# A first sequence in blocks of 112 consecutive tokens: convolution by tap matrices and a router in the same layout

## Chip, cores, metric

One core of one Trainium2 chip. The metric is the device time of one execution in microseconds (us). Chips differ: the first comparison ran on a chip where the kernel before takes 1368 us; of the three chips of the experiments, chip 11 takes the same 1368, chips 2 and 10 take 1382 to 1383. Each experiment is therefore held against runs of the kernel before on its own chip.

## The reference, cut

```python
# 8 sequences of 3584 tokens, 192 channels; depthwise causal convolution,
# 7 taps, one set of taps per head of 24 channels
w = exp(w - max(w)); w = w / (sum(w) + 1e-9)
y[b, s, h] = sum_k w[h, k] * x_pad[b, s + k, h]
# mixture of 8 experts; a token takes over the expert of the token before it
logits = y @ w_gate
local  = sigmoid(y @ w_local)
e = argmax(logits[s]) if s == 0 or local[s] < 0.5 else e_of_token(s - 1)
out[s] = softmax(logits[s])[e] * (relu(y[s] @ w1[e]) @ w2[e])
```

## The kernel before: the parts concerned

The 28,672 tokens are cut into 16 groups of 1792; two groups are one sequence. A group is convolved and routed, its rows are scattered to slots sorted by expert, and a loop over blocks of slots reads them back, multiplies and scatters the results. Before the loop come groups 0 and 1. There a partition holds 14 tokens in a row; four of eight heads are convolved by TensorE with diagonal matrices, one matmul per tap, the rest by VectorE.

```python
for i, h in enumerate(ON_PE):                     # 4 heads x 7 taps
    for k in range(KC):
        ...                                       # cut: i == 0, the same on VectorE
        nc.scalar.activation(dg_of(i, k), ident, Act.Copy, scale=c[:, h, k:k + 1])
...
for k in range(KC):                               # 28 matmuls of 336 columns
    nc.tensor.matmul(acc, lhsT=dg_of(i, k), rhs=chans(h, k),
                     start=(k == 0), stop=(k == KC - 1))
...
for k in range(1, KC):                            # the other heads
    nc.vector.scalar_tensor_tensor(cols(h), chans(h, k), c[:, h, k:k + 1],
                                   cols(h), Alu.mult, Alu.add)
```

The loop; `step(t)` issues about `t` us of VectorE work for later groups (convolution, router):

```python
xT, _ = turn(blocks[0][1], xgs[0])                # transposes of slot rows
for i, (_, n, _, _) in enumerate(blocks):
    ensure(i)                                     # slot rows ahead
    weights(i + AHEAD)                            # expert weights ahead
    hT = hidden(n, wbs[i], xT)                    # H_i
    xT, copied = turn(blocks[i + 1][1], xgs[i + 1])
    ...                                           # cut: a scatter of a later group
    step(2.5 if n == 1 else 4.2)
    output(n, wbs.pop(i), xgs.pop(i), hT)         # O_i, then step(1.2), then o_sb
    step(1.3 if n == 1 else 3.0)
```

`output` takes two PSUM tiles (PSUM is the memory that matmuls write to); the next `output` can start only when VectorE's `o_sb` has read them, and VectorE works in program order.

Of the kernel before, what the change touches and what calls it, by code (L numbers as in the profile page):

```python
# [17 lines left out]
P = 128  # L18
# [6 lines left out]
NT = 14  # L25
# [3 lines left out]
NP = NT // 2  # L29
HALO = KC - 1  # L30
NX = NT + HALO
# [24 lines left out]
GQ = (NP + 3) // 4  # L56
# [17 lines left out]
def taps(nc, scr, w):  # L74

    wm = scr.tile([1, H], F32, name="wm")
    nc.vector.tensor_reduce(wm, w, axis=AX.X, op=Alu.max)
    nc.vector.tensor_tensor(w, w, bcast(wm, KC), op=Alu.subtract)
    nc.scalar.activation(w, w, Act.Exp)
    ws = scr.tile([1, H], F32, name="ws")  # L80
    nc.vector.tensor_reduce(ws, w, axis=AX.X, op=Alu.add)
    nc.vector.tensor_scalar(ws, ws, 1e-9, None, Alu.add)
    nc.vector.reciprocal(ws, ws)
    nc.vector.tensor_tensor(w, w, bcast(ws, KC), op=Alu.mult)


@with_exitstack
def kernel(
    ctx: ExitStack,
    tc: tile.TileContext,  # L90
    x: bass.AP,
    weight: bass.AP,
    wgl: bass.AP,
# [31 lines left out]

    ident = cst.tile([P, P], F32, name="ident")
    ones = cst.tile([P, P], F32, name="ones")
    c = cst.tile([P, H, KC], F32, name="c")
    with tc.tile_pool(name="scr", bufs=1) as scr:
        w = scr.tile([1, H, KC], F32, name="w")  # L130
        nc.scalar.dma_start(out=w, in_=weight.rearrange("(o h) k -> o h k", o=1))
        x_in = {0: load_x(0)}
        nc.gpsimd.memset(ones, 1.0)
        any_ = scr.tile([1, 1], F32, name="any_")
        nc.scalar.activation(any_, ones[:1, :1], Act.Exp)
        make_identity(nc, ident)
        taps(nc, scr, w)
        cps = hps_p.tile([P, GQ * P], F32, name="hps")
        nc.tensor.matmul(cps[:, :H * KC], lhsT=ones[:1, :], rhs=w.rearrange("o h k -> o (h k)"),
                         start=True, stop=True)  # L140
        nc.vector.tensor_copy(c.rearrange("p h k -> p (h k)"), cps[:, :H * KC])
    wg = cst.tile([P, 3 + DQ, Q], F32, name="wg")
    nc.sync.dma_start(out=wg.rearrange("p k e -> p (k e)"), in_=wgl)
    wgq = wg[:, 3:, :]
    x_in[1] = load_x(1)


    HEADS = [5, 6, 7, 0, 1, 2, 3, 4]
    ON_PE = HEADS[:4]
    got = {}  # L150


    diag = wp.tile([P, WA + WB], F32, name="wb")

    def dg_of(i, k):
        n = i * KC + k
        return diag[:, n * P:(n + 1) * P] if n < 24 else more[:, (n - 24) * P:(n - 23) * P]

    more = wp.tile([P, WA + WB], F32, name="wb")
    for i, h in enumerate(ON_PE):  # L160
        for k in range(KC):
            if i == 0:
                nc.vector.tensor_scalar(dg_of(i, k), ident, c[:, h, k:k + 1], None, Alu.mult)
            else:
                nc.scalar.activation(dg_of(i, k), ident, Act.Copy, scale=c[:, h, k:k + 1])

    def conv(g, x_sb, on_pe=(), alone=False):

        y_sb = ys.tile([P, NT, DG], F32, name="y_sb")
        got[g] = y_sb  # L170

        def cols(h):
            return y_sb[:, :, Y0 + h * GS:Y0 + (h + 1) * GS]

        def chans(h, k):
            return x_sb[:, k:k + NT, h * GS:(h + 1) * GS]

        def first(h):
            if alone:
                nc.vector.tensor_scalar(cols(h), chans(h, 0), c[:, h, 0:1], None, Alu.mult)  # L180
            else:
                nc.scalar.activation(cols(h), chans(h, 0), Act.Copy, scale=c[:, h, 0:1])  # L182

        def others():
            for i, h in enumerate(on_pe):
                cps = (yps_p.tile([P, 512], F32, name="yps") if g else
                       hps_p.tile([P, 512], F32, name="hps"))
                acc = cps[:, :NT * GS]
                for k in range(KC):
                    nc.tensor.matmul(acc, lhsT=dg_of(i, k), rhs=chans(h, k),  # L190
                                     start=(k == 0), stop=(k == KC - 1))
                    if k == KC - 1:
                        nc.scalar.copy(cols(h), acc.rearrange("p (t d) -> p t d", d=GS))
                    yield

        def mine():
            hs = [h for h in HEADS if h not in on_pe]
            if not alone:
                first(hs[0])
                yield 0  # L200
            for i, h in enumerate(hs):
                if alone:
                    first(h)
                elif i + 1 < len(hs):
                    first(hs[i + 1])
                for k in range(1, KC):
                    nc.vector.scalar_tensor_tensor(cols(h), chans(h, k), c[:, h, k:k + 1],  # L207
                                                   cols(h), Alu.mult, Alu.add)
                    yield 0.6

        return mine(), others()

    for gen in reversed(conv(0, x_in.pop(0), ON_PE, True)):
        for _ in gen:
            pass
# [23 lines left out]
    i_of = pf[:, 0:1]  # L239
    so_far = cst.tile([1, P + 1], F32, name="so_far")  # L240
    nc.gpsimd.memset(so_far, 0.0)
    lsb = cst.tile([P, GQ * P], F32, name="lsb")
# [6 lines left out]
    for zero in (lsb, rk, bk, mk, mc, tq):  # L249
        nc.gpsimd.memset(zero, 0.0)  # L250
# [32 lines left out]
    def wide_logits(g, y_sb):  # L283

        zy = yt.tile([P, NT * DR + 12 * 2 * P], F32, name="z")
        yr = zy[:, :NT * DR].rearrange("p (t d) -> p t d", d=DR)
        yT = zy[:, NT * DR:].rearrange("p (u j x) -> p u j x", u=3, j=4)

        copy = nc.scalar.copy if g else nc.gpsimd.tensor_copy
        copy(yr, y_sb[:, :, Y0 + P:Y0 + D])  # L290
        if not g:
            copy(y_sb[:, :, Y0 + D:], y_sb[:, :, Y0:Y0 + DR])



        for u in range(3):
            tps = [hps_p.tile([P, 4 * GQ, DR], F32, name="hps") for half in range(2)]
            for j in range(4):
                for q in range(GQ):
                    t = min(2 * (4 * q + j), NT - 2)  # L300
                    src = (yr[:, t:t + 2, :].rearrange("p t d -> p (t d)") if u == 2
                           else y_sb[:, t + u, Y0:Y0 + P])
                    for half in range(2):
                        turn_half(tps[half][:, GQ * j + q, :], src, half)
            for half in range(2):
                to = yT[:, u, :, :].rearrange("p j (q s) -> p (j q) s", q=GQ)
                leave = nc.vector.tensor_copy if g == 0 and half else nc.scalar.copy
                leave(to[:, :, half * DR:(half + 1) * DR], tps[half])
        lps = hps_p.tile([P, 2 * P], F32, name="hps")
        for u in range(3):  # L310
            for j in range(4):
                w = (2 if 4 + j < NP else 1) * P
                nc.tensor.matmul(lps[32 * j:32 * j + 32, :w], lhsT=wg[:, u, :],
                                 rhs=yT[:, u, j, :w], start=(u == 0), stop=(u == 2))
        m = 32 * (NP - 4)
        nc.scalar.copy(lsb[:m, :], lps[:m, :])
        nc.scalar.copy(lsb[m:, :P], lps[m:, :P])
        if g:
            copy(y_sb[:, :, Y0 + D:], y_sb[:, :, Y0:Y0 + DR])
        yield "hop"  # L320
        ltp = [hps_p.tile([P, GQ, 2, 32], F32, name="hps") for half in range(2)]
        for q in range(GQ):
            for half in range(2):
                turn_half(ltp[half][:, q, :, :].rearrange("p j e -> p (j e)"),
                          lsb[:, q * P:(q + 1) * P], half)
        lt = sm.tile([P, NT + 2, E + 1], F32, name="lt")
        yield "pe"
        for half in range(2):
            nc.vector.tensor_copy(
                lt.rearrange("p (q h j u) e -> p q h j (u e)", q=GQ, h=2, u=2)[:, :, half, :, :],  # L330
                ltp[half][:, :, :, :2 * (E + 1)])
        return lt

    def logits(g, y_sb):

        nc.gpsimd.tensor_copy(y_sb[:, :, Y0 + D:], y_sb[:, :, Y0:Y0 + DR])
        zy = yt.tile([P, NT * DR + 12 * 2 * P], F32, name="z")
        z = zy[:, :NT * D].rearrange("p (t d) -> p t d", d=D)
# [32 lines left out]

    def route(g, alone):
        y_sb = got.pop(g)
        lt = yield from (wide_logits if alone else logits)(g, y_sb)
        lg = lt[:, :NT, :E]
        mx = sm.tile([P, NT], F32, name="mx")
        nc.vector.tensor_reduce(mx, lg, axis=AX.X, op=Alu.max)
# [169 lines left out]
        if ONE[g] > (ONE[was] if g else 0):  # L547
            yield from table(0, g, 1, ONE[g])
# [415 lines left out]
```

## Time and profile before

| | kernel before |
|---|---|
| time, median of the first 3 runs | 1368.14 us |
| span of the profiled run | 1366.1 us |
| TensorE (PE) busy from 330 us on | 1029.4 of 1030 us |
| slot numbers of group 0 (T0) | 46.7 us |
| first hidden products H0 | 71.6 us |
| second output products O1, third hidden products H2 | 84.7, 87.4 us |

How to read it: from 330 us on PE has no gap, so a change of the part before the loop can move the end only by what it changes before 330 us. What is called "lead" below is the difference of two traces in the start of the same copy of a transposed block (there are 142 copies, one per block), each counted from its span's start. The trace lists each matmul here as two records, which the counts (x32) count.

The waits of PE between 75 and 130 us show what disturbs these first blocks (columns: engine, line, releaser, us in total, times, longest). Slot rows come late by 3.6 us, and nothing waits for VectorE's `o_sb`:

```profile
PE xps L279 <- DMA xg<-slots: 3.6, 2, 2.4
PE yps L760 <- issue: 1.7, 1, 1.7
```

### The profile page before, as it was taken

The page shows a single profiled execution, that of the slowest core. Times are in us where ns is not written, and L with a number is a line of the kernel's source. Part 1 is how long each engine was busy: PE and PEld are TensorE (multiplying, and loading weights), DVE is VectorE, ACT ScalarE, POOL GpSimd, SP SyncE. Part 2 cuts the span into 40 slices and gives each one's busy share as a digit, 9 for nine tenths or more (in the row PEclk, how much of TensorE's full clock was granted, in tenths as well). Part 3 has the DMA queues.
Part 4 walks back from the last instruction along what each step waited for, and adds up shares of the span by engine and source line. Part 5 has one row for each costly group of instructions (what it writes and reads, how often), then busy time and mean ns, then how long its engine had stood idle before and what let it go on. Part 6 is the DMA issues. An engine that isn't in the chain of part 4 may idle for free. (4 is left out here: it accounts for less than half of the span.)

```text
span 1366.1 us, 41871 instructions
## 1 busy us (share of the span) xinstructions
PE 1327.2 (97%) x17142; PEld 1252.3 (92%) x17142; DVE 795.1 (58%) x2459; ACT 512.1 (37%) x1146; POOL 481.2 (35%) x513
## 2 busy tenths in 40 slices
PE   6789999999999999999999999999999999999998
PEld 4488999999999999999999999999999999999997
DVE  6778999988878777878686868684500000000000
ACT  3243444434333333333343434333333333333333
POOL 1442444434343434344444344443343111112111
PEclk9989999999999999999999999999999999999999
DMA  4399999996675757676767676565566555556893
GB/s 181 102 375 374 374 390 373 359 353 251 235 273 206 267 208 265 213 264 219 264 228 265 223 266 220 208 211 208 212 221 224 202 196 181 181 178 235 318 325 131
DMA packets 65812, 340.75 MB, mean 249 GB/s; under 512 B 12369, under 2 KB 23240, under 8 KB 45395
## 3 DMA queue, kind: packets, MB, share of 16 engines
q1 hardware_dynamic: 43488, 285.35, 57.8%
q0 software_dynamic: 22128, 52.70, 10.2%
q8 instruction: 136, 2.23, 0.7%
q14 instruction: 58, 0.47, 0.1%
q10 hardware_dynamic: 2, 0.00, 0.0%
HBM read 285.20 MB, written 53.29 MB: 248 GB/s over the span
## 5 line engine op out<-in xcount | busy, mean ns | idle before, releaser
L760 PE MATMUL yps<-wb,hT 64*128 64x192 f32 x7328 | 636.9, 325 | 3.7 <-DVE o_sb L772 2.0
L744 PE MATMUL hps<-xT,wb 64*128 64x256 f32 (+1 forms) x6816 | 630.4, 337 | 0.8 <-ACT xT L730 0.6
L760 PEld LDWEIGHTS yps<-wb,hT 64*128 64x128 f32 x7328 | 599.7, 187 | 8.5 <-issue 4.5
L744 PEld LDWEIGHTS hps<-xT,wb 64*128 64x128 f32 x6816 | 567.1, 188 | 41.5 <-issue 1.1
L776 POOL DMA_INDIRECT out_dram<-o_sb,xg x229 | 231.5, 1011 | 664.3 <-DVE o_sb L772 591.6
L207 DVE SCALAR_TENSOR_TENSOR y_sb<-x_sb,c,y_sb 128x336 f32<-128x336 f32 x720 | 406.2, 573 | 28.5 <-ACT y_sb L182 9.3
L749 ACT ACTIVATE hT<-hps 128x512 f32<-128x512 f32 (+1 forms) x568 | 261.3, 512 | 361.2 <-PE hps L744 361.0
L772 DVE SCALAR_TENSOR_TENSOR o_sb<-yps,xg,o_sb 128x192 f32<-128x192 f32 x229 | 87.2, 412 | 488.6 <-ACT o_sb L768 488.6
L567 POOL DMA_INDIRECT slots<-y_sb,posi x224 | 222.7, 994 | 185.7 <-ACT hT L749 92.2
L768 ACT ACTIVATE o_sb<-yps,xg 128x192 f32<-128x192 f32 x229 | 87.0, 419 | 420.6 <-PE yps L760 417.0
L730 ACT COPY xT<-xps 128x768 f32<-128x768 f32 (+1 forms) x142 | 96.7, 681 | 11.6 <-PE xps L279 11.6
L279 PEld LDWEIGHTS xps<-ident,xg 64*128 64x128 f32 x1374 | 71.2, 140 | 13.8 <-issue 3.9
L279 PE MATMUL xps<-ident,xg 64*128 64x64 f32 x1374 | 72.5, 222 | 5.8 <-DMA xg<-slots 5.8
L182 ACT ACTIVATE y_sb<-x_sb,c 128x336 f32<-128x336 f32 x116 | 66.7, 586 | 0.0
L341 DVE STREAM_TRANSPOSE z<-y_sb 128x768 f32<-128x768 f32 (+1 forms) x56 | 45.5, 853 | 0.5
L367 DVE COPY lt<-lq 32x36 f32<-32x36 f32 x224 | 41.6, 186 | 3.5
L351 PE MATMUL hps<-z,wg 64*32 64x128 f32 x1344 | 26.7, 274 | 1.4 <-DVE z L341 1.3
L351 PEld LDWEIGHTS hps<-z,wg 64*32 64x32 f32 x1344 | 20.7, 105 | 5.0 <-DVE z L341 3.0
L190 PE MATMUL hps<-x_sb,wb 128*128 128x336 f32 x56 | 18.9, 506 | 4.0 <-DMA x_sb<-in_x_dram 4.0
L190 PEld LDWEIGHTS hps<-x_sb,wb 128*128 128x128 f32 x56 | 12.1, 218 | 10.5 <-issue 6.2
L190 PE MATMUL yps<-x_sb,wb 128*128 128x336 f32 x56 | 16.8, 451 | 0.0
L190 PEld LDWEIGHTS yps<-x_sb,wb 128*128 128x128 f32 x56 | 10.3, 190 | 4.5
(165 smaller groups left out, 336.0 us busy)
## 6 DMA issues: line engine op xcount, KB each, us to landing
wb<-in_w_dram SPq DMA_DIRECT2D x142, 1536.0 KB
x_sb<-in_x_dram SPq DMA_DIRECT2D x16, 1920.0 KB
xg<-slots SPq DMA_DIRECT2D x87, 258.0 KB
xg<-slots SPq DMA_DIRECT2D x55, 129.0 KB
out_dram<-o_sb,xg POOLq DMA_INDIRECT x229
slots<-y_sb,posi POOLq DMA_INDIRECT x224
wg<-in_wgl_dram SPq DMA_DIRECT2D x1, 144.0 KB
slots<-pad SPq DMA_DIRECT2D x1, 129.0 KB
```

The lines of the kernel that those rows point to most:

```text
L182: nc.scalar.activation(cols(h), chans(h, 0), Act.Copy, scale=c[:, h, 0:1])
L190: nc.tensor.matmul(acc, lhsT=dg_of(i, k), rhs=chans(h, k), start=(k == 0), stop=(k == KC - 1))
L207: nc.vector.scalar_tensor_tensor(cols(h), chans(h, k), c[:, h, k:k + 1], cols(h), Alu.mult, Alu.add)
L279: nc.tensor.transpose(to, src[rows], identity=ident[rows, rows])
L567: ins = nc.gpsimd.indirect_dma_start(out=slots[:, :], in_=rows, in_offset=None, out_offset=bass.IndirectOffsetOnAxis(ap=to, axis=0)).ins
L730: copied = nc.scalar.copy(to, at)
L744: nc.tensor.matmul(hps[half][:, j, w], lhsT=wb[rows, f0:f0 + P], rhs=xT[rows, d, w], start=(d == 0 and j == 0), stop=(d == KD - 1), skip_g ...
L749: relu = nc.scalar.activation(hT[:, m:m + 2, w], hps[half][:, :, w], Act.Relu)
L760: nc.tensor.matmul(yps[half][:, k * D:(k + 1) * D], lhsT=hT[rows, m, k * P:(k + 1) * P], rhs=wb[rows, WA + m * D:WA + (m + 1) * D], start= ...
L768: nc.scalar.activation(o_sb[:, k, :], y[k][0], Act.Copy, scale=xg[:, k, 0:1])
L772: nc.vector.scalar_tensor_tensor(o_sb[:, k, :], y[k][1], xg[:, k, 0:1], o_sb[:, k, :], Alu.mult, Alu.add)
L776: sent = nc.gpsimd.indirect_dma_start(out=out, in_=o_sb[:, k, :], in_offset=None, out_offset=bass.IndirectOffsetOnAxis(ap=xg.bitcast(I32)[ ...
```

## The change

Intent: both groups of the first sequence in blocks of 112 consecutive tokens, 16 blocks side by side, a block's tokens along the partitions. A convolution of one head is then one product with a 118x112 tap matrix in place of seven with diagonal matrices, and no head is left to VectorE; the router's scans run along rows. The tap matrices come from the host as unnormalized logarithms (-1e30 off the band) and are exponentiated on chip. Further, ahead of the loop, `step(15)` starts group 2's convolution on VectorE. Core of the diff:

```diff
+        nc.scalar.dma_start(out=hank, in_=wh)          # tap matrices, second queue
+        x_in = {0: load_b(0)}                          # x in blocks, two halves
...
+        for h in range(H):
+            nc.scalar.activation(hank[:, h, :], hank[:, h, :], Act.Exp, bias=nm[:, h:h + 1])
+        ... normalization: exp(w), sums, 1/sums on VectorE, then a matmul that spreads them
+        nc.tensor.matmul(cps[:, :H + H * KC], lhsT=ones[:1, :], rhs=ws, start=True, stop=True)
+        nc.vector.tensor_copy(rz, cps[:, :H])
...
-    for gen in reversed(conv(0, x_in.pop(0), ON_PE, True)):
+        for b0 in (0, NH):
+            for h in range(H):                         # 16 matmuls of 192 columns a group
+                nc.tensor.matmul(ps, lhsT=hank[:NI, h, :],
+                                 rhs=xv[:NI, b0:b0 + NH, h * GS:(h + 1) * GS],
+                                 start=True, stop=True)
...  (cut: logits with whole transposes, router along rows, 16 scatters a group in place of 14)
+    for _ in wide_route(1, yb, acc[1]):
+        step(1.2)
-    for _ in range(4):
+    for _ in range(6):
         put()
+    step(15)
     AHEAD = 3
```

## The prediction

> **What bounds the kernel now.** I read, in this order, the page's slices, the busy time by stretch, TensorE's waits by stretch, and the timeline of the first 130 us. The chain that ended last is of no use: it holds only the last output scatter (0.1%).
>
> The slices come first. TensorE (PE) is at 9 from the fourth slice on; only the first three (34 us each) have room. GpSimd and ScalarE are never near full; DMA is at 9 in slices 3 to 8.
> ```profile
> PE   6789999999999999999999999999999999999998
> DVE  6778999988878777878686868684500000000000
> PEclk9989999999999999999999999999999999999999
> DMA  4399999996675757676767676565566555556893
> ```
> Next the stretches (start:end, then busy us of PE, PE weight load, VectorE, ScalarE, GpSimd, then clock, DMA share, GB/s). After 330 us PE is busy 1029.4 of 1030 us, and its waits there list nothing: that stretch only shifts. Between 62 and 76 us PE is mostly idle or at half clock.
> ```profile
> 62.00:72.00 10.00, 2.76 (x15) 1.98 (x17) 8.34 (x43) 0.78 (x2) 4.18 (x5) 0.51 0.53 159
> 72.00:76.00 4.00, 4.00 (x40) 4.00 (x40) 1.02 (x8) 0.66 (x2) 3.00 (x4) 0.51 0.94 360
> 76.00:82.00 6.00, 6.00 (x98) 5.94 (x94) 2.55 (x5) 3.04 (x8) 2.52 (x3) 1.00 1.01 397
> 330.00:1360.00 1030.00, 1029.38 (x13003) 978.44 (x13000) 515.98 (x1617) 380.70 (x804) 350.41 (x352) 1.00 0.65 230
> ```
> So the end is set by when the expert loop starts and by PE's stalls early in it. The timeline (start, duration, engine, line) gives the chain to the loop: convolution from 8.67, logits from 28.19, slot numbers of group 0 (`posi`) at 46.56, fourteen scatters from 47.67 to 64.61, the read of the slots at 68.41, the first transposes at 70.48, the first hidden product at 71.64.
> ```profile
> 8.67 18.94 PE L190 MATMUL hps<-x_sb,wb 128*128 128x336 f32 x56 [3.98 <-DMA x_sb<-in_x_dram]
> 28.19 1.22 PE L279 MATMUL hps<-ident,y_sb 64*128 64x64 f32 x32 [0.57 <-issue]
> 46.56 0.17 DVE L539 CAST posi<-pos 128x14 int32<-128x14 f32 x1
> 47.67 1.27 POOL L567 DMA_INDIRECT slots<-y_sb,posi  x1 [18.58 <-issue]
> 64.61 0.96 POOL L567 DMA_INDIRECT slots<-y_sb,posi  x1 [0.30 <-issue]
> 68.41 1.19 SPq L697 DMA_DIRECT2D xg<-slots  x2
> 70.48 0.59 PE L279 MATMUL xps<-ident,xg 64*128 64x64 f32 x6 [2.27 <-DMA xg<-slots]
> 71.64 4.98 PE L744 MATMUL hps<-xT,wb 64*128 64x128 f32 x48 [0.57 <-ACT xT L730]
> 79.94 0.42 DVE L772 SCALAR_TENSOR_TENSOR o_sb<-yps,xg,o_sb 128x192 f32<-128x192 f32 x1 [1.19 <-ACT o_sb L768]
> 80.28 5.87 DVE L207 SCALAR_TENSOR_TENSOR y_sb<-x_sb,c,y_sb 128x336 f32<-128x336 f32 x10
> 84.51 0.40 PE L279 MATMUL xps<-ident,xg 64*128 64x64 f32 x6 [2.37 <-DMA xg<-slots]
> 84.72 2.85 PE L760 MATMUL yps<-wb,hT 64*128 64x192 f32 x32
> ```
> Call posi's end T0 (46.7 before) and the k-th block's hidden products Hk, its output products Ok. Undisturbed, a block takes 5.52 us (H8 to H9, 126.98 to 132.49). H0 to H7 (71.64 to 121.43) took 49.8 us instead of 7x5.52+1.9 (logits of group 2)=40.5: about 9 us of stalls and half clock.
>
> **What the Trainium skill says.** "TensorE: Matmul & The Clock Gate", Part 1: after an idle window of about 3.4 us PE falls to half clock and needs about as long a busy one to return. The trace agrees in part: H0 took 4.98 us at 0.51, H1 2.84 at full clock. But PE was at full clock at 8.67, after eight idle microseconds. Same page, Part 2, "Step-by-step": MATMULs stay in program order, only weight loads are pulled ahead; the trace shows it where O1 waits behind the transposes at 84.51. "ScalarE: Activation LUTs", "What ACT_TABLE_LOAD costs": an ACTIVATE with a pointer operand takes 280 ns + 0.833 ns per element and overlaps its neighbour by 93 ns; at 128 columns an estimated 294 ns, and the trace has 21 in 6.24 us (297 ns).
>
> **The change, part by part.** Groups 0 and 1 (one sequence, 3584 tokens) both get the new layout. In the main loop the instruction orders of both kernels hold the same products and logits; what changes is the prologue and where group 2's convolution lies.
>
> *Taps.* The tap matrices (459 KB, second queue) and half of x (786 KB) come together. Before, 1.92 MB of x landed at 8.5 us; by share of bytes I estimate 5.7 for the taps. Then, on one chain: 8 exponentials of 112 columns at 0.28 (2.25), the exponential of w (0.25), four small VectorE operations (0.9 as at 3.03 to 3.91 before), hops (0.2), a matmul (0.67). This matmul is ahead of the convolution in PE's order, so the convolution starts at 10.0, later than before (8.67), and its evacuation needs `rz` at 10.3.
>
> *Convolution of group 0.* 28 matmuls of 336 columns (0.555 each on PE, 18.9 us with VectorE's share beside) become 16 of 192: 0.555x192/336=0.32, say 0.33; 5.3 us. Evacuation by two engines, about 0.35 each, keeps pace. Done at 15.3 against 27.6.
>
> *Logits.* 24 whole transposes in lots of four (0.5 us a lot, estimated from 32 half ones in 1.22), evacuation 0.45 to 0.5 a lot, wide products 1.8 per half, then copies, four transposes, one copy: about 7.8 us; the 8.4 before (28.1 to 36.5) were similar. Logits at 23.1.
>
> *Router.* 33 VectorE operations; spaced as in the undisturbed chain of group 1 before (61.47 to 69.61), 9.3 us. Group 1's convolution lies between on PE; of the four PSUM buffers the counting matmul needs one that ScalarE must first empty: +1.1. T0=33.5, 13.2 us earlier.
>
> *Scatters.* 16 instead of 14 at 1.27 us spacing, on the path: T0 to H0 was 24.9, becomes 27.5 (24.9+2x1.27). H0=61.0 against 71.64: 10.6 us gained so far.
>
> *What gives part of it back: VectorE.* In the new order group 2's convolution is issued ahead: four pairs inside group 1's router, then 33 operations in a row before the first `o_sb` of the loop. Group 1's logits come at T0+8.6 (its convolution is emptied by ScalarE alone), its router takes 9.3 plus six of those operations, less one covered hop: 12.4, so posi of group 1 at T0+21. Then two operations (1.15), the bases and table (4.3), 33 operations at 0.585 (10 took 5.87; 19.3) and `o_sb` (0.45): T0+46.2=79.7. O1 needs the PSUM that this `o_sb` frees. PE would be at O1 at 61.0+13.1=74.1 (as 71.64 to 84.72), so it waits about 5.6 us more, and falls to half clock: about 1.9 us, as H0 lost 2.1. H2=79.7+2.7+1.9=84.3 against 87.37: the 10.6 has become 3.1. After that VectorE is ahead: group 2's logits follow after O1 nearly without a wait, and H7 comes at 84.3+0.4+1.9+5x5.52=114.2, say 115.5 with small stalls, against 121.43. From there both are PE bound: 6 us gained, 1368.1-6=1362.
>
> **The rivals.**
> (a) *PE goes cold in the prologue.* It has less work there; at half clock the convolution takes up to 3 us longer, logits 2 to 4, router 1. For: the drop at about 62 us before, with PE lightly used. Against: full clock at 8.67 and through 28 to 36 us, where it was half idle. The end would be about 1366.
> (b) *VectorE does not hold O1 back*, because group 1 is routed sooner than I think. Then nearly all 10.6 us stay, plus some of the old stall at 84.51: 1356. Against: the order of VectorE's instructions, 33 in a row, is fixed.
> (c) *DMA is the bound at the loop's start.* The share is 1.01 at 76 to 82 us and about 1 till 200. Then an earlier loop would just wait for weights. Against: PE's waits for DMA from 75 to 130 us are 3.6 us in all and none later, and the loads start earlier too. 1364.
> (d) *Nothing gained*: the two extra scatters, the later start and the held O1 eat all, 1368 to 1371.
>
> **Range and chances.** The prologue has 71 us in all; a change of 2% is 27 us, which even a free convolution would not give. So "same" is nearly sure. My main sum gives 1362; (a) and (c) pull up by 2 to 4, (b) down by 6. T0 carries some 3 us of uncertainty, the return by VectorE some 4. Range 1354 to 1369; faster by 2%: 0.01, same 0.98, slower 0.01.
>
> **What would show each step right or wrong.** First convolution matmul near 10 us, right after the tap normalization; 0.33 us per matmul; posi of group 0 near 33.5; 16 scatters spaced about 1.27; H0 near 61; `o_sb` of block 0 behind a row of 33 convolution operations, ending near 80, with PE waiting for it; H7 near 115; the waits after 330 us empty as before. Wrong: a clock near 0.5 at 10 to 30 us (a), no wait of O1 for VectorE (b), transposes waiting on slot reads where O1 waited (c), or a difference that arises after 330 us, which would overthrow the whole picture.

## The result, and the profile after

| | before | after | predicted after |
|---|---|---|---|
| median us (4 runs each, one chip) | 1368.22 | 1369.76 | 1362.0 |
| T0 | 46.7 | 38.95 | 33.5 |
| H0 | 71.6 | 65.5 | 61.0 |
| O1 | 84.7 | 84.3 | 79.7 |
| H2 | 87.4 | 88.4 | 84.3 |
| H7 | 121.4 | 119.3 | 115.5 |
| span of the profiled run | 1366.1 | 1367.0 | |

The ratio is 1.0015, 95% interval 0.9997 to 1.0032: the same time, 0.76 us above the range. Ratios here and below are the mean time of one kernel's fast runs over that of the other's of the same rounds, so not quite the ratio of the medians quoted.

The slices of the page after. PE has more room in the first three slices than before, VectorE (DVE) less work in the first, and the clock is lower in the second:

```profile
PE   5479999999999999999999999999999999999997
DVE  3799999988787878777878787865000000000000
PEclk9789999999999999999999999999999999999999
```

The same stretches as in the prediction (start:end, then busy us of PE, PE weight load, VectorE, ScalarE, GpSimd, then clock, DMA share, GB/s). From 62 to 76 us PE now works where it stood or ran at half clock before, but from 76 to 82 it is busy only 1.17 of 6 us, while VectorE is busy 5.72. From 330 us on nothing changed:

```profile
62.00:72.00 10.00, 7.12 (x74) 6.94 (x76) 9.33 (x27) 2.20 (x7) 5.67 (x7) 0.56 0.92 304
72.00:76.00 4.00, 4.00 (x66) 4.00 (x64) 3.79 (x8) 1.51 (x4) 1.00 (x1) 1.00 1.04 421
76.00:82.00 6.00, 1.17 (x16) 0.71 (x14) 5.72 (x11) 1.14 (x3) 0.00 (x0) 0.91 1.03 433
330.00:1360.00 1030.00, 1030.00 (x12948) 978.74 (x12944) 501.15 (x1552) 379.73 (x800) 349.43 (x346) 1.00 0.64 228
```

The timeline of the new chain (start, duration, engine, line, in brackets the idle time before and what ended it):

```profile
8.43 2.34 ACT L154 ACTIVATE wb<-wb,nm 128x112 f32<-128x112 f32 x8 [4.70 <-DMA wb<-in_wh_dram]
11.85 0.68 PE L164 MATMUL hps<-ws,ones 1*128 1x64 f32 x2 [8.66 <-DVE ws L162]
12.46 7.24 PE L179 MATMUL hps<-x_sb,wb 118*112 118x192 f32 x32
38.78 0.17 DVE L435 CAST posi<-pos 112x16 int32<-112x16 f32 x1
39.91 1.16 POOL L657 DMA_INDIRECT slots<-y_sb,posi  x1 [18.46 <-issue]
58.83 0.94 POOL L657 DMA_INDIRECT slots<-y_sb,posi  x1 [0.30 <-issue]
61.82 1.20 SPq L787 DMA_DIRECT2D xg<-slots  x2
65.47 5.44 PE L834 MATMUL hps<-xT,wb 64*128 64x128 f32 x48 [0.57 <-ACT xT L820]
64.59 19.31 DVE L346 SCALAR_TENSOR_TENSOR y_sb<-x_sb,c,y_sb 128x336 f32<-128x336 f32 x33
83.82 0.41 DVE L862 SCALAR_TENSOR_TENSOR o_sb<-yps,xg,o_sb 128x192 f32<-128x192 f32 x1
77.92 0.54 PE L850 MATMUL yps<-wb,hT 64*128 64x192 f32 x2
84.28 4.41 PE L850 MATMUL yps<-wb,hT 64*128 64x192 f32 x29 [5.82 <-DVE o_sb L862]
```

The first exponential waits 4.70 us for the tap matrices and starts at 8.43; the convolution then takes 7.24 us. The 33 convolution operations of group 2 stand on VectorE ahead of the first `o_sb`; O1 had begun at 77.92 with two of its 32 records and waits 5.82 us for it. When it goes on, it takes 4.41 us for 29 records where a whole output takes 2.82 at full clock: the clock had dropped again.

So 6.2 us of lead at H0 became a lag of 1.0 at H2. After H2 the lead comes back to 2.1 us at H7: group 2's logits, which are earlier now, lengthen one block by 3.3 us (H2 to H3), where they lengthened one by 6.1 (H6 to H7 before; 5.52 undisturbed). Then about 3 us are lost in pieces, each around the logits of a later group. At copies before which both kernels have done the logits of the same groups, the lead is 2.1 us at block 8 (123 us), 0.4 at block 16 (173 us), -0.3 at block 25 (227 us), -0.9 at block 34 (283 us) and -0.6 at the last. The waits of PE between 130 and 330 us, first before, then after:

```profile
PE yps L760 <- DVE o_sb L772: 2.0, 7, 0.6
PE hps L351 <- DVE z L341: 0.9, 2, 0.5
```
```profile
PE hps L463 <- DVE z L453: 2.2, 4, 0.8
PE hps L834 <- issue: 2.0, 2, 1.0
```

The dearest of these logits are those at 250 us, which wait three times for VectorE's `z` and then run in part at half clock. They take 5.18 us in all; the same group's took 2.92 in the kernel before:

```profile
249.66 0.41 PE L463 MATMUL hps<-z,wg 64*32 64x128 f32 x4 [0.57 <-DVE z L453]
250.43 0.41 PE L463 MATMUL hps<-z,wg 64*32 64x128 f32 x4 [0.36 <-DVE z L453]
251.61 3.23 PE L463 MATMUL hps<-z,wg 64*32 64x128 f32 x88 [0.78 <-DVE z L453]
```

### The profile page after: what moved, and what is told of

It reads as the page before. It is cut to its first block, busy times and chain, and to the rows that moved or that the text cites. A ratio compares the mean times of both kernels' runs of the same rounds, so it can differ in the third digit from the quotient of the medians.

```text
span 1367.0 us, 41654 instructions
## 1 busy us (share of the span) xinstructions
PE 1315.4 (96%) x17048; PEld 1249.1 (91%) x17048; DVE 779.1 (57%) x2420; ACT 511.0 (37%) x1145; POOL 489.2 (36%) x522
## 5 line engine op out<-in xcount | busy, mean ns | idle before, releaser
L834 PEld LDWEIGHTS hps<-xT,wb 64*128 64x128 f32 x6816 | 564.9, 188 | 45.3 <-issue 4.5
L346 DVE SCALAR_TENSOR_TENSOR y_sb<-x_sb,c,y_sb 128x336 f32<-128x336 f32 x672 | 385.1, 584 | 46.5 <-ACT y_sb L338 28.8
L657 POOL DMA_INDIRECT slots<-y_sb,posi x228 | 230.6, 1011 | 196.7 <-ACT hT L839 113.8
L318 PEld LDWEIGHTS xps<-ident,xg 64*128 64x128 f32 x1374 | 68.9, 140 | 17.9 <-DMA xg<-slots 8.6
L338 ACT ACTIVATE y_sb<-x_sb,c 128x336 f32<-128x336 f32 x112 | 62.7, 585 | 0.0
L179 PE MATMUL hps<-x_sb,wb 118*112 118x192 f32 x64 | 14.7, 397 | 0.7 <-ACT y_sb L187 0.6
L468 ACT COPY ls<-hps 128x128 f32<-128x128 f32 x28 | 6.1, 269 | 23.1 <-PE hps L463 23.1
L179 PEld LDWEIGHTS hps<-x_sb,wb 118*112 118x112 f32 x64 | 13.3, 224 | 1.4 <-ACT y_sb L187 0.8
L449 POOL COPY y_sb<-y_sb 128x896 f32<-128x896 f32 x14 | 13.2, 941 | 0.1
```

The costliest lines, as they stand in the source:

```text
L318: nc.tensor.transpose(to, src[rows], identity=ident[rows, rows])
L338: nc.scalar.activation(cols(h), chans(h, 0), Act.Copy, scale=c[:, h, 0:1])
L657: ins = nc.gpsimd.indirect_dma_start(out=slots[:, :], in_=rows, in_offset=None, out_offset=bass.IndirectOffsetOnAxis(ap=to, axis=0)).ins
L834: nc.tensor.matmul(hps[half][:, j, w], lhsT=wb[rows, f0:f0 + P], rhs=xT[rows, d, w], start=(d == 0 and j == 0), stop=(d == KD - 1), skip_g ...
```

## The experiments

Fifteen runs: e1 to e4 on chip 2, e5 to e8 on chip 10, f1 to f4 and g1 to g3 on chip 11. The theory: the end follows the loop's start, so what the prologue lacks (late tap matrices, long order of operations, cold clock) and what VectorE's row of group 2 holds back are what is missing. The rivals: DMA bounds the loop's start; group 2's early work is free, as it must be done anyway.

| run | edit to the changed kernel | median us (runs) | before, same chip | ratio [95%] |
|---|---|---|---|---|
| e1_again | none | 1401.72 (4) | 1383.11 | 1.0139 [1.0123, 1.0154] |
| e2_no_early | no `step(15)` | 1382.27 (5) | 1383.11 | 0.9998 [0.9985, 1.0012] |
| e3_norm_first | normalization first | 1396.31 (4) | 1383.11 | 1.0102 [1.0087, 1.0118] |
| e4_taps_first | tap load first | 1397.22 (4) | 1383.11 | 1.0107 [1.0091, 1.0122] |
| e5_before | (the kernel before) | 1382.5 (1) | 1382.05 | |
| e6_all | all three | 1378.09 (5) | 1382.05 | 0.9968 [0.9954, 0.9981] |
| e7_warm | e6 + idle products | 1377.8 (6) | 1382.05 | 0.9969 [0.9953, 0.9985] |
| e8_weights | e6 + weights first | 1381.0 (5) | 1382.05 | 0.9988 [0.9975, 1.0001] |
| f1_after | none | 1370.1 (6) | 1367.77 | 1.0013 [1.0000, 1.0025] |
| f2_no_early | no `step(15)` | 1361.74 (6) | 1367.77 | 0.9962 [0.9940, 0.9983] |
| f3_half | `step(7)` | 1361.16 (6) | 1367.77 | 0.9956 [0.9942, 0.9970] |
| f4_best | e7, 8 idle products for 10 | 1355.56 (6) | 1367.77 | 0.9906 [0.9890, 0.9922] |
| g1_start | tap load and normalization first | 1364.23 (6) | 1367.9 | 0.9973 [0.9959, 0.9986] |
| g2_all | = e6 | 1356.44 (5) | 1367.9 | 0.9914 [0.9898, 0.9930] |
| g3_half_warm | f4 + `step(7)` | 1354.55 (4) | 1367.9 | 0.9895 [0.9874, 0.9916] |

### On chip 2: e1 to e4

`e1_again` is the changed kernel, unedited.

> The changed kernel itself once more, on the chip of the other runs of this lot. Both theories: 1368.5 to 1371, within 0.3% of the kernel before. A second trace tells what of the loss after the first blocks is regular: theory A (the prologue's chain sets the start and VectorE's 33 convolution operations hold the second block's outputs at 84 us; what is lost after block 7 is regular) expects the half-clock stretch near 250 us and the gaps near 149 and 203 us again; if they are chance, they lie elsewhere or are gone, and the span moves by 1 to 2 us.

`e2_no_early`:
```diff
-    step(15)
     AHEAD = 3
```

> The changed kernel without the 25 convolution operations of group 2 that are issued before the expert loop (8 operations inside group 1's router stay). Theory A, VectorE holds the second block's outputs: they start at about 78 instead of 84.3 us, held by the slot rows' DMA, the half clock at 79 to 85 us is gone, and the end comes 4 to 6 us earlier, about 1364. Theory B, the lead is lost later anyway, because what the early operations did must be done inside the first blocks and group 2's logits or the DMA then bind: the second block is as early as A says, but the end moves by less than 1.5 us, about 1369.

`e3_norm_first` (the loop of eight exponentials moved behind the matmul of the normalization):
```diff
-        for h in range(H):
-            nc.scalar.activation(hank[:, h, :], hank[:, h, :], Act.Exp, bias=nm[:, h:h + 1])
         ws = scr.tile([1, H + H * KC], F32, name="ws")
         ...
         nc.vector.tensor_copy(c.rearrange("p h k -> p (h k)"), cps[:, H:H + H * KC])
+        for h in range(H):
+            nc.scalar.activation(hank[:, h, :], hank[:, h, :], Act.Exp, bias=nm[:, h:h + 1])
```

> The changed kernel with the tap normalization (exponential of w, four VectorE operations, the broadcasting matmul) issued ahead of the eight exponentials of the tap matrices. The normalization is then done while the tap matrices are still loading. Both theories of the prologue: first convolution matmul at about 9.0 instead of 12.46 us, slot numbers of group 0 at about 35.5 instead of 38.95. Theory A: everything after shifts with it, end 3 us earlier, about 1366.5. Theory B: the end stays within 1 us of the changed kernel.

`e4_taps_first`:
```diff
-        nc.scalar.dma_start(out=hank, in_=wh)
+        nc.sync.dma_start(out=hank, in_=wh)
         x_in = {0: load_b(0)}
```

> The changed kernel with the tap matrices loaded first on the queue of x instead of on the second queue beside it. If the 8.43 us at which the first exponential starts comes from sharing the DMA engines with 3.1 MB of x, the first exponential starts at about 5 us, the first convolution matmul at about 9.5, slot numbers of group 0 at about 36, and by theory A the end is about 3 us earlier, 1366.5; by theory B it stays. If the queue has nothing to do with it, the first exponential stays at about 8.4.

Measured: on this chip the changed kernel is 1.4% slower than before, not equal. Without the early convolution it is equal to before: that one line costs 19 us here. The two edits of the start move T0 (the end of `posi`) from 39.3 to 36.0 (e3) and 34.9 (e4), 3.3 and 4.4 us, and the times by 5.4 and 4.5 us (3 were expected of each). The end follows the start; a bound by DMA at the loop's start would have eaten that.

Why 19 us here and 1.5 there was open. The waits of VectorE between 20 and 130 us in e1 list two with "remote", a release that no engine of this core gave, ahead of group 1's router; the row of 33 then begins at 72.07, not at 64.59, and O1 comes at 91.76, although H0 (65.28) is as early as on the first chip:

```profile
DVE wb L240 <- remote: 5.4, 1, 5.4
DVE lt L245 <- remote: 2.4, 1, 2.4
```
```profile
65.28 5.49 PE L834 MATMUL hps<-xT,wb 64*128 64x128 f32 x48 [0.58 <-ACT xT L820]
72.07 19.31 DVE L346 SCALAR_TENSOR_TENSOR y_sb<-x_sb,c,y_sb 128x336 f32<-128x336 f32 x33
91.76 4.27 PE L850 MATMUL yps<-wb,hT 64*128 64x192 f32 x29 [6.51 <-DVE o_sb L862]
```

e2 has the same two stalls and loses nothing by them, as its O1 does not wait for VectorE. With the early row on the path, a stall of VectorE ahead of it is on the path too. By the traces this accounts for most of the difference between the chips: at block 8 e1 is 13.5 us behind e2, where f1 (chip 11, below) is 6.6 behind f2. At the last block it is 17.0 against 8.3; what the rest is, no run tells.

### On chip 10: e5 to e8

`e5_before` is the kernel before, for its trace on a chip of this kind.

> The kernel before, unchanged, only to have its trace from the same chip as the next three. All theories: a time equal to its own runs here; first transposed block copied at about the same 71 us after the start as on the first chip, and the clock low until about 14.5 us.

A miss: the first block was copied at 79.3 us, 8 later than on the first chip; the clock's first record is at 14.1, much as there (14.5). ScalarE has "remote" waits of its own here:

```profile
ACT z L308 <- remote: 10.5, 2, 6.1
ACT hT L749 <- remote: 4.7, 1, 4.7
```

So ScalarE's stalls are not the change's; the kernel before has them too on this kind of chip. VectorE's "remote" waits are in all seven traces of the changed kernel on chips 2 and 10 and not in e5, the only trace there of the kernel before.

`e6_all` joins e2, e3 and e4.

> The changed kernel with the three repairs that were each tried alone: tap matrices loaded first, normalization ahead of the eight exponentials, and no early convolution of group 2 ahead of the loop. Theory A (the end follows the prologue, and the early convolution is what gave the gain back): the two prologue savings (2.7 and 4.0 us at the first block) add up less what x's first half makes binding, 5 to 6.5 us, and the end is 4 to 7 us under that of the variant without early convolution, so ratio 0.995 to 0.997 against the kernel before. Rival B (the loop's start is bound by DMA, so an earlier start only waits longer): ratio 0.999 to 1.001, the 5 us reappearing as waits of transposes and products for weights or slot rows before 90 us.

`e7_warm` (to e6):
```diff
+        idle = hps_p.tile([P, 512], F32, name="hps")
+        for _ in range(8):        # behind the copy to nm
+            nc.tensor.matmul(idle[:, :P], lhsT=ident, rhs=ident, start=True, stop=True)
...
+    for _ in range(10):           # ahead of the first turn()
+        nc.tensor.matmul(idle[:, :288], lhsT=ident, rhs=wg.rearrange("p k e -> p (k e)"),
+                         start=True, stop=True)
```

> The same with idle products that keep TensorE busy before the first convolution and before the first expert block. If the low clock is what made the convolution and the first hidden products slow: convolution products every 0.33 us instead of 0.45 to 0.64, first hidden products 2.8 instead of 5.4 us; first block 1.5 to 2.5 us earlier than the run without idle products, hidden products done 4 to 5 us earlier. End: theory A 2 to 4 us under that run, ratio 0.992 to 0.995. Rival B: the same end within 1 us, because the second block then waits for its slot rows instead.

`e8_weights` (to e6):
```diff
-    weights(0)
+    weights(AHEAD - 1)
     for j in range(2):
         xgs[j] = load_rows(j)
-    weights(AHEAD - 1)
```

> The variant with all repairs, and the second and third expert's weight loads issued ahead of the first slot reads, which wait for the scatters in the same queue. Theory: if the stalls after the first block are waits for weights that were issued late, they shrink from some 7 us to under 3 and the end is 2 to 4 us earlier than without, ratio 0.992 to 0.995. Rival: the DMA engines are full anyway between 40 and 100 us, then the loads take share from the scatters and slot rows, the first block comes 0 to 2 us later, and the end is unchanged or later.

Measured: e6 is at 0.9968, at the edge of what was expected, and no rival's 0.999. e7 warmed the convolution (5.45 us for its 16 products in place of 7.65), but its time is e6's: a miss of 2 to 4 us. Its first block was copied at 61.30 us, 1.7 later than e6's, where 1.5 to 2.5 earlier was expected; the ten idle products ahead of the loop ended only as the first transposes began (60.85). e8 is some 3 us slower than e6: its first block came 1.4 us later, as its rival said, and its PE still waits 2.5 us at "issue" and 2.3 for slot rows between 60 and 130 us. Late weights were not the cause of the stalls after the first block.

A thing of these chips stays open. In e6, e7 and e8 a lead over e5 of 12.7, 16.5 and 14.6 us at block 44 shrinks to 2.8, 6.8 and 3.5 at block 98. Between blocks 44 and 92 one block takes 11.13 us in the kernel before on either kind of chip and 11.12 in the changed kernel on the first chip, but 11.26 to 11.34 in all seven runs of the changed kernel on chips 2 and 10. Between 400 and 600 us, and again between 600 and 800, their traces show five to twelve distances of 0.3 us or more between two starts on PE; the other traces have four or fewer. Most of the waits that the profile lists there are put down to "issue". It would explain why e2 only equals before. What stalls PE there, and why only with the changed kernel's instructions, no run tells.

### On chip 11: f1 to f4

The chip where the kernel before takes 1367.8 us, as in the first comparison. `f1_after` is the changed kernel; `f2_no_early` is e2; `f3_half` has `step(7)` in place of `step(15)`; `f4_best` is e7 with 8 idle products in place of 10 ahead of the loop.

> The changed kernel again, as the anchor of the next three. If the long ScalarE and VectorE stalls without a releaser (4 to 10 us each within the first 100 us in every earlier experiment, none in the first pair of traces) belong to the chip, then: on a chip that shows them about 1.4% over the kernel before, on one that doesn't 0.1 to 0.2% over it. Rival: they come at random; then this run's times scatter between the two.

> The changed kernel without the group-2 convolution ahead of the loop, again. On a chip with the stalls: 18 to 20 us faster than the changed kernel, equal to before. On a chip without them: the hold of the second block's output products by VectorE (5.8 us of wait and about 2 us of half clock) is all there is to gain, less what the later logits of group 2 cost: 3 to 6 us faster than the changed kernel, 0.996 to 0.999 of before. Rival (the early convolution costs nothing where VectorE isn't stalled, since its work must be done anyway): equal to the changed kernel within 1 us.

> The changed kernel with a third to a half of that early convolution (a step of 7 in place of 15): 13 to 14 fewer operations of 0.585 us, about 8 us, ahead of the first output accumulation. If that row on VectorE is what holds the second block's output products, the hold of 5.8 to 6.5 us vanishes entirely and the time is that of the variant without early convolution within 2 us. Rival (the harm is that group 2's logits come early and interrupt the first blocks): about half of the difference remains.

> All repairs with the idle products, two fewer of them ahead of the first block (8 in place of 10, some 1.5 us less). Expected to be the fastest: first hidden products 0 to 1.5 us earlier than with ten, ratio 0.995 to 0.998 of before. If the clock was kept only by the last ones, the first hidden products fall to half clock and the gain is lost.

f1 gives 1.0013, the 1.0015 of the first comparison, and no "remote" wait: the stalls belong to the chip. f2 is 8.4 us faster than f1, more than the 3 to 6 expected (I had counted on late logits of group 2 costing something; f2's products of them, 1.59 us at full clock, were cheaper than f1's, 2.53). The row ahead of the first `o_sb` shrinks to seven operations, VectorE waits for ScalarE and not PE for VectorE, and O1 comes at 79.39 (f1: 85.13):

```profile
65.94 4.06 DVE L346 SCALAR_TENSOR_TENSOR y_sb<-x_sb,c,y_sb 128x336 f32<-128x336 f32 x7
74.59 0.42 DVE L862 SCALAR_TENSOR_TENSOR o_sb<-yps,xg,o_sb 128x192 f32<-128x192 f32 x1 [4.59 <-ACT o_sb L858]
79.39 4.53 PE L850 MATMUL yps<-wb,hT 64*128 64x192 f32 x32
```

f3 keeps 19 of the 33 in the row. Its `o_sb` is ready at 76.7, before PE asks (78.49), and the whole gain is there, 8.9 us, although group 2's logits still come early. Not the early logits cost, but the row's length on VectorE:

```profile
65.25 11.13 DVE L346 SCALAR_TENSOR_TENSOR y_sb<-x_sb,c,y_sb 128x336 f32<-128x336 f32 x19
76.30 0.41 DVE L862 SCALAR_TENSOR_TENSOR o_sb<-yps,xg,o_sb 128x192 f32<-128x192 f32 x1
78.49 2.84 PE L850 MATMUL yps<-wb,hT 64*128 64x192 f32 x32
```

The waits of PE from 62 to 130 us say it in one line, first f1, then f3, where no wait for `o_sb` is left:

```profile
PE xps L318 <- DMA xg<-slots: 11.3, 2, 8.1
PE yps L850 <- DVE o_sb L862: 4.8, 2, 4.6
```
```profile
PE xps L318 <- DMA xg<-slots: 9.0, 2, 8.0
PE hps L834 <- ACT xT L820: 0.6, 1, 0.6
```

What the 8 to 9 us are made of, from f1 against f3: O1 at 85.13 against 78.49 (6.6), then 4.5 us to the start of H2 against 2.7, as the clock had dropped meanwhile (1.8), so H2 at 89.63 against 81.15 (8.5).

f4 is at 0.9906, 14.5 us under f1 and better than expected. In it the first hidden products ran at full clock (2.95 us; 5.44 in the changed kernel) but, unlike in e7, not the convolution, with the same instructions before it. Neither is assured: in g3 (below), with the same idle products, it is the other way round, 5.45 us for the convolution and 4.50 for the first hidden products. First e7 (chip 10), then f4:

```profile
7.39 5.45 PE L182 MATMUL hps<-x_sb,wb 118*112 118x192 f32 x32
```
```profile
7.44 7.30 PE L182 MATMUL hps<-x_sb,wb 118*112 118x192 f32 x32
```

### On chip 11: g1 to g3

`g1_start` has the edits of e3 and e4 and keeps `step(15)`; `g2_all` is e6; `g3_half_warm` is f4 with `step(7)`.

> The changed kernel with the early start alone repaired (tap matrices loaded first, normalization ahead of the exponentials), the early convolution of group 2 kept. If the prediction failed by its start alone: group 0's slot numbers at 33 to 34 us, second block's output products at 79 to 80, still waiting 4 to 6 us for VectorE, and the time 5 to 6 us under the changed kernel, that is 1362 to 1365 where the kernel before takes 1368 (ratio 0.996 to 0.998); on a chip where the kernel before takes 1382, about 1.008. Rival (what is gained at the start is lost at the hold): slot numbers as early, but the time within 2 us of the changed kernel, ratio 1.000 to 1.002.

> The start repaired and the early convolution left out, no idle products. Theory: the two gains add: 5 to 6 us under the variant that only left out the early convolution, ratio 0.991 to 0.993; the idle products were worth no more than 1 to 2 us of the 0.9906. Rival: the idle products before the first block were what gained, then this run is at 0.995 to 0.996. On a slow chip 0.997 as before.

> The start repaired, idle products, and the short early convolution (a step of 7). If a row of 19 operations is still too long for the earlier first block: output products of the second block wait for VectorE 1 to 2 us and the time is equal to that of the run without (0.990 to 0.992). If the gain seen with the short row (about 3 us in the trace, 0.6 us in the times) is real: 0.988 to 0.990.

g1 gives the changed kernel the start that was predicted, and it gains about what was predicted for that start: 1364.23 us, 5.9 under f1, though still 2.2 over the 1362 of the prediction. The chain of g1:

```profile
4.02 2.34 ACT L166 ACTIVATE wb<-wb,nm 128x112 f32<-128x112 f32 x8 [0.24 <-DMA wb<-in_wh_dram]
6.80 7.11 PE L179 MATMUL hps<-x_sb,wb 118*112 118x192 f32 x32 [1.11 <-DMA x_sb<-in_xb_dram]
32.97 0.17 DVE L435 CAST posi<-pos 112x16 int32<-112x16 f32 x1
78.43 4.39 PE L850 MATMUL yps<-wb,hT 64*128 64x192 f32 x29 [5.56 <-DVE o_sb L862]
```

The tap matrices no longer wait (0.24 us), `posi` ends at 33.1 where 33.5 was predicted, O1 waits 5.56 us and resumes at 78.43 where 79.7 was predicted. Against f1 all of g1 is shifted and nothing else: the lead is 6.2 us at the first of the 142 copies, 7.3 at the last, and between 5.2 and 7.3 at each of them. The rival, that the hold takes the start's gain too, is out, since the hold moves with the start.

g2 has both repairs: 13.7 us under f1, and the parts add up (5.9 + 8.4 = 14.3). The idle products of f4 give 0.9 us at most, inside the scatter. g3 is the fastest, 1354.55, but not told apart from f4 or g2. These three beat both kernels by about 1%.

## Why the prediction was wrong, step by step

It predicted a gain of 6.2 us (1368.22 to 1362.0) and measured was a loss of 1.5; the miss is 7.8 us. Two steps failed: T0, and the claim that the lead of the first blocks is kept from there on.

- *Taps landed at 5.7.* Wrong: 8.43. Estimated by share of bytes among loads running together; f1, f2 and f3 show 8.5 to 8.9. Issued ahead of x, the same load lets the exponentials start at 4.0 (g1). "DMA: Bandwidth & Descriptors", section "Issuing engines are not separate DMA queues", of the Trainium skill says that starting transfers from another engine saves only issue time, as all run on the same 16 engines and interleave. That agrees: the second queue gave the small, urgent load no precedence (the edit of g1 changes its queue and its place together). The convolution starts at 12.46 in place of 10.0, 2.5 us of T0.
- *Convolution in 5.3 us at full clock from the start.* Wrong: 7.24. I read "full clock at 8.67" in the trace before from a clock column that had no record there: clock records begin at 14.5 us before and at 16.1 after, and the page prints 1.00 until then. Counting products tells it. In the trace before, PE was busy throughout both of these stretches, but made half as many in the first (columns: busy us and count, clock, DMA share, GB/s):

```profile
9.00:14.00 5.00, 5.00 (x10) 1.00 0.76 303
15.00:20.00 5.00, 5.00 (x19) 1.00 0.00 0
```

  The prediction's own cost had a sign of it: 28 matmuls at 0.555 us are 15.5 us, not the 18.9 of the line. "TensorE: Matmul & The Clock Gate", Part 1, of the Trainium skill says that the default state is the throttled one; the prediction quoted the page and set this trace against it wrongly. 1.9 us, rival (a) in part; that these 1.9 us would arrive at the end, no run shows: e7 won them, but its first block came later than e6's all the same. With 0.3 us for the logits and 0.8 for the router, T0 is 5.4 us late.
- *16 scatters at 1.27, T0 to H0 27.5.* Right in kind, 26.5 measured (starts 1.26 apart on average); 1.0 us in favour.
- *VectorE's row holds O1 to T0+46.2, half clock costs 1.9.* Right: T0+45.3 in the result, and g1, from its own T0, has 78.43 where T0+46.2 gives 79.3. The half clock cost 1.9 in the result (29 records in 4.41 us; at full clock 2.82 x 29/32 = 2.56). Rival (b), no hold, is out.
- *H7 at 115.5.* 119.3, that is 3.8 late: T0's 5.4, less 1.0 and 0.6 for small differences.
- *From there both are PE bound and keep 6 us.* Wrong by about 3 us: the lead of 2.1 at H7 is a lag of 0.9 in span at the end. The places are shown above, the passages around later logits between 125 and 285 us; f1 and g1 lose at the same ones. The prediction's working has no reading of 130 to 330 us but the 9 of the slices, and a 9 leaves up to a tenth of each slice open: PE was busy 196.81 of these 200 us before and 195.01 after. Why the changed kernel loses more there isn't settled by an experiment.
- *Rival (c), DMA as the bound.* Out on chip 11, where most of what is won ahead of the loop arrives at the end (g1 against f1: 6.2 us at the first copy, 7.3 at the last; g2 against f2: 7.6 and 5.6). PE's waits for slot rows grew to 9.5 us, nearly all the wait for the first ones, which ends with the scatters. Rival (d), nothing gained, gave the right number, and two of its three causes: the later start and the held O1; the extra scatters were counted in the sum anyway.

Two terms were mis-sized then, T0 (5.4 us) and the late blocks (about 3). Given T0, g1 has H0 at 59.9 and O1 at 78.4, about 1 us before the predicted times, and H7 at 113.5, 2 before. That its end comes within 2.2 us of 1362 is in part luck, as this and the late loss have opposite signs. What the prediction saw but did not ask: the held O1 was the dearest part of the change, 8 to 9 us, by one line with no need to be there (shown by f2 and f3).

## What to carry to other kernels

An engine with slack on average can still hold the bottleneck: count how many of its operations stand, in program order, ahead of the one that frees the bottleneck's buffer, and size early work so that this row ends before the buffer is asked for (19 operations here, not 33). A small load that heads a chain is issued ahead of big ones, not on another queue beside them. And read a clock column at the start of a trace by counting products per us, as it may print a value where nothing was recorded.

## What the Trainium skill lacked or had wrong

- "TensorE: Matmul & The Clock Gate", Part 1: right that cold is the default, and the runs agree with its statement that the window runs freely, so that equal programs differ: the same convolution behind the same idle products took 7.30 us in f4, but 5.45 in g3 on the same chip. It warns of unreliable clock events, but not that a profile may print 1.00 ahead of the first record (14.5 us before, 16.1 after), where the products show half clock.
- "DMA: Bandwidth & Descriptors": it says that transfers of several queues interleave and how queues take turns, but has no time to landing for a small load beside larger ones. Here 459 KB beside larger loads let its reader start at 8.4 to 8.9 us; issued first, at 4.0.
- On no page that I read: chips of one kind differ. The kernel before took 1368 us on chip 11, 1383 and 1382 on chips 2 and 10. There ScalarE has waits of up to 7.7 us without a releaser on the core in every trace, and VectorE in most; on chip 11 neither in any trace.
- On no page that I read: the time GpSimd needs per indirect scatter. 0.96 us with 128 rows and 0.94 with 112 (medians; starts 1.26 and 1.25 apart), so that fewer rows bought almost nothing, and with two scatters more group 0's took 19.9 us from first to last in place of 17.9.
